# Retention on one core: scores in 64x64 products, q decayed on GpSimd, results copied by ScalarE

## The chip, the cores and the metric

One core of a Trainium2 chip. The metric is device microseconds (us) of one execution. Engines: PE is TensorE, with PEld its weight loads; DVE is VectorE, ACT is ScalarE, POOL is GpSimd; SP is SyncE, which issues all loads and stores of this kernel. Each engine works through its own instructions in the order in which the kernel emits them, and waits for the others by semaphores.

## The reference

```python
q, k, v                                   # (4, 8, 576, 64): batch, heads, positions, head size
gamma = 1 - 2.0 ** (-5 - arange(8))       # one decay for each head
scores = q @ k^T / sqrt(64)
ret = scores * where(i >= j, gamma ** (i - j), 0)
x = (ret @ v)                             # -> (2304, 512), heads side by side
h = x @ w_in                              # 512 -> 2048
y = (h * sigmoid(1.702 * h)) @ w_out      # 2048 -> 512
h2 = y @ w2_in                            # 512 -> 1024
u = h2 * softmax(h2); u = layernorm(u) * g_ln
out = u @ w2_out                          # 1024 -> 512
```

All of it in float32. The change touches the retention (up to `x`) and the order in which the weights of `w_in` and `w_out` are loaded.

## The kernel before, in words

The program works in three parts: retention, the first network (`emit_h`, `emit_y`), the second network. The change lies in the first.

*Units.* Retention is cut into 16 units: 4 batches of 4 pairs of heads. The two heads of a pair lie one in partitions 0 to 63 and one in 64 to 127 wherever the head's 64 elements are the partitions. A unit holds q and k transposed (head element by position), k and v by position, in 4 chunks of 128 positions and a last one of 64. Inside a chunk, scores are computed, masked by the triangle and multiplied with v. Between chunks, what is before is carried by a state of 64x64 for each head. The decay `gamma ** (i - j)` is split in two factors: v is scaled by `gamma ** -j` (`st0`, three ACT instructions, L304 and L305), and in the kernel before the results are multiplied by `gamma ** i` on DVE when they leave PSUM (L402 for 512 positions, L407 for the last 64).

*Steps of a unit.* `st2`: scores on PE (L351), then masked by DVE into r1 (L355, one instruction for each head). `states`: products of k and v on PE (L316), scaled on their way out by ACT (L322). `st1`: the states are accumulated over the chunks by one scan on DVE (L331). `last_scores`: scores of the last 64 positions (L339) and their mask (L340). `st4`: results from the masked scores (L372), from the states (L384, L390) and from the last positions (L395), and the two DVE instructions into x.

*Order.* It is written out by hand (`run`, L647), and the scheduler keeps it. Iteration u of the loop of L699 emits `st2(u)`, then `st4(u - 1)` with `states(u)` and `last_scores(u)` inside, the load of unit u + 4 into the buffer just freed (5 buffers, `NU`), half a weight slice if u is even, `st1(u)` and `st0(u + 2)`. In iterations 1 to 4 `split_x` cuts the first block of x into a rounded part (ACT, L423) and a rest (POOL, L424), 384 positions for each of four units.

*Weights.* Each of 8 slices of the first network comes as two halves of 512 KB in a wide format (`load_w`), is converted by 6 DVE instructions (`convert`: L226, L229, L232, twice) and split into a rounded part (ACT, L249) and a rest (POOL, two L254). This is the background work: one piece of DVE in each iteration above 3, two in even ones. The splits follow at once behind a slice's last conversion, which is in iterations 7, 11 and 15. The first network runs in three generations over its slices (0 to 2, 3 to 7, 8 to 15), each over 5 blocks of positions; the first `h` product (L443) comes in iteration 16, ahead of the last unit's `st4`.

*PSUM.* Two groups of 4 banks: one for the scores, one for states and results.

Of the kernel before, what the change touches and what calls it, by code (L numbers as in the profile page):

```python
# [13 lines left out]
ALU = mybir.AluOpType  # L14
# [3 lines left out]
B, H, S, D = 4, 8, 576, 64  # L18
NP = H // 2
# [4 lines left out]
P = 128  # L24
CH = 128
NCH = 4
# [12 lines left out]
FB = F2 // P  # L39


CQK, CQ2, CK2 = 0, NCH * 2 * CH, NCH * 2 * CH + LAST
CKN, CV = 2 * S, 2 * S + NCH * P
NV = 2 * NCH + 1
CATT = CV + NV * D
# [55 lines left out]
_M = {}  # L101
# [8 lines left out]
CMEM = _n  # L110


NU = 5
IN_AT = [_M["att"], _M["att"] + CATT] + [_M["y"] + i * CATT for i in range(3)]
ST_AT = _M["att"] + 2 * CATT
R1_AT = ST_AT + 2 * NCH * D
R2_AT = R1_AT + 4 * NCH * CH
# [30 lines left out]
class Build:  # L148
# [53 lines left out]
        lo, hi = _CC[name]  # L202
        return self.at(_M["c"] + lo, hi - lo)

    def load_unit(self, u, part=None):

        t = IN_AT[u % NU]
        a, b = {None: (0, CATT), 0: (0, 2 * CH), 1: (2 * CH, CKN), 2: (CKN, CATT), 3: (0, CKN)}[part]
        self.load(t + a, self.att_in[u, :, a:b])

    def load_raw(self, dst, src):
# [76 lines left out]
    def ybank(self, name):  # L288
        return self.ps.tile([P, 512], F32, tag="y", name=name, bufs=4)

    def q(self, t, c, rows=slice(0, P)):
        return t[rows, CQK + 2 * c * CH:CQK + (2 * c + 1) * CH] if c < NCH else t[rows, CQ2:CQ2 + LAST]

    def k(self, t, c, rows):
        return t[rows, CQK + (2 * c + 1) * CH:CQK + (2 * c + 2) * CH] if c < NCH else t[rows, CK2:CK2 + LAST]

    def st0(self, u):

# [34 lines left out]
    def last_scores(self, u, s):  # L333

        nc = self.nc
        t, _, _, r2 = self.un(u)
        for a in range(2):
            r = slice(a * D, (a + 1) * D)
            nc.tensor.matmul(s[r], self.k(t, NCH, r), self.q(t, NCH, r), start=True, stop=True)  # L339
        return lambda: nc.vector.tensor_tensor(r2, s, self.const("tri2"), ALU.mult)  # L340

    def st2(self, u):

        nc = self.nc
        t, _, r1, _ = self.un(u)
        s = [self.ybank(f"s_{u}_{a}") for a in range(2)]

        for c in range(NCH):
            for a in range(2):
                r = slice(a * D, (a + 1) * D)  # L350
                nc.tensor.matmul(  # L351
                    s[a][:, c * CH:(c + 1) * CH], self.k(t, c, r), self.q(t, c, r), start=True, stop=True
                )
        for a in range(2):
            nc.vector.tensor_tensor(  # L355
                r1[a], s[a].rearrange("r (c i) -> r c i", c=NCH),
                self.const("tri").unsqueeze(1).to_broadcast([P, NCH, CH]), ALU.mult,
            )
        if u == 0:
            self.last_scores(0, self.bank("s2")[:, 0:LAST])()  # L360

    def st4(self, u):

        nc = self.nc
        t, st, r1, r2 = self.un(u)
        o = self.bank(f"o1_{u}")
        half = [slice(a * D, (a + 1) * D) for a in range(2)]


        for c in range(NCH):  # L370
            for a, r in enumerate(half):
                nc.tensor.matmul(  # L372
                    o[r, c * CH:(c + 1) * CH],
                    t[:, CV + c * P + a * D:CV + c * P + (a + 1) * D],
                    r1[a][:, c],
                    start=(c == 0), stop=False, skip_group_check=True,
                )

        if u + 1 < B * NP:
            self.states(u + 1)  # L380

        for c in range(1, NCH):
            for r in half:
                nc.tensor.matmul(  # L384
                    o[r, c * CH:(c + 1) * CH], st[r, c - 1], self.q(t, c, r),
                    start=False, stop=(c == NCH - 1), skip_group_check=True,
                )
        o2 = self.bank(f"o2_{u}")
        for r in half:
            nc.tensor.matmul(  # L390
                o2[r, 0:LAST], st[r, NCH - 1], self.q(t, NCH, r),
                start=True, stop=False, skip_group_check=True,
            )
        for r in half:
            nc.tensor.matmul(  # L395
                o2[r, 0:LAST], t[r, CV + NCH * P:CATT], r2[r],
                start=False, stop=True, skip_group_check=True,
            )
        mask = self.last_scores(u + 1, o2[:, LAST:2 * LAST]) if u + 1 < B * NP else None
        n = NCH * CH  # L400
        d = self.const("qdec")[:, u % NP * CH:(u % NP + 1) * CH]
        nc.vector.tensor_tensor(  # L402
            self.x(u)[:, 0:n].rearrange("r (c i) -> r c i", c=NCH),
            o[:, 0:n].rearrange("r (c i) -> r c i", c=NCH),
            d.unsqueeze(1).to_broadcast([P, NCH, CH]), ALU.mult,
        )
        nc.vector.tensor_tensor(self.x(u)[:, n:S], o2[:, 0:LAST], d[:, 0:LAST], ALU.mult)  # L407
        if mask:
            mask()

# [236 lines left out]
    def run(self):  # L647
# [14 lines left out]
        def load_w():  # L662
            if raws:
                f, h = raws.pop(0)
                n = slice(h * SLICE, (h + 1) * SLICE)
                self.load_raw(self.wraw[f][:, n], self.w1_in[f][:, h * DM:(h + 1) * DM])

        for part in range(3):
            self.load_unit(0, part)
            if part == 0:  # L670
                self.load_consts()
        self.fill_scan()
        self.load_decays(0, 1)
        self.load_unit(1, 3)
        self.load_unit(1, 2)
        self.load_decays(1, NP - 1)
        for u in range(2, NU):
            self.load_unit(u, 3)
            self.load_unit(u, 2)
        load_w()  # L680
        load_w()

        for f in range(FH):
            t = T_START[f % 2]
# [5 lines left out]


        last = B * NP - 1
        self.st0(0)
        self.st0(1)
        self.st2(0)
        self.states(0)
        self.st1(0)
        self.st0(2)
        for u in range(1, last + 2):  # L699
            if u <= last:  # L700
                self.st2(u)
                if u > 3:
                    self.background(1)
            else:

                while 0 not in self.split:
                    self.background(1)
                self.emit_h(0, 0, 0, nc.vector, True)
            self.st4(u - 1)
            self.staged.add((4, u - 1))  # L710

            if u - 1 + NU <= last:
                self.load_unit(u - 1 + NU)
            if u % 2 == 0:
                load_w()
            if u <= last:
                self.st1(u)
            if u < last - 1:
                self.st0(u + 2)
            if u > 3 and u % 2 == 0:  # L720
                self.background(1)
            if u - 1 < NP:
                self.split_x(0, 0, u - 1)
# [169 lines left out]
def layout(q, k, v, moe_w_in, moe_w_out, moe2_w_in, moe2_w_out, moe2_g_ln):  # L893
# [4 lines left out]
    nat = lambda a: rows(a).transpose(0, 1, 3, 2, 4).reshape(B * NP, S, P)  # L898
    kn, vn = nat(k), nat(v)
    n = NCH * P  # L900
    chunks = lambda a: a[:, :, :n].reshape(-1, P, NCH, CH)
    qk = np.stack([chunks(tr(q)), chunks(tr(k))], 3)
    att[:, :, CQK:CQ2] = qk.reshape(-1, P, 2 * n)
    att[:, :, CQ2:CK2], att[:, :, CK2:CKN] = tr(q)[:, :, n:], tr(k)[:, :, n:]
    for at, a in ((CKN, kn), (CV, vn)):
        att[:, :, at:at + n] = a[:, :n].reshape(-1, NCH, P, P).transpose(0, 2, 1, 3).reshape(-1, P, n)
    for a in range(2):
# [35 lines left out]
```

## Time and profile before

| | |
|---|---|
| median of 3 runs | 676.5 us (676.45 to 676.79) |
| the profiled execution | 676.72 us |
| its span, first to last instruction | 674.8 us |
| PE busy | 666.7 us, 4070 products |
| PEld busy | 580.0 us |
| DVE busy | 494.4 us |
| ACT busy | 233.2 us |
| POOL busy | 235.8 us |
| moved by DMA | 49.34 MB |

The profile comes from one execution. "Busy" counts the time in which an engine works on an instruction; PE's products overlap each other in its pipeline, so that a busy PE need not be at its peak. A row of the timeline gives the start, the duration and the engine, then line, operation, what is written and read, and how many instructions were merged; in brackets the idle time before it and what ended it. A float32 product shows as two records on PE, so `x16` in L351 is 8 products.

### The profile page before, as it was taken

The page shows a single profiled execution, that of the slowest core. Times are in us where ns is not written, and L with a number is a line of the kernel's source. Part 1 is how long each engine was busy: PE and PEld are TensorE (multiplying, and loading weights), DVE is VectorE, ACT ScalarE, POOL GpSimd, SP SyncE. Part 2 cuts the span into 40 slices and gives each one's busy share as a digit, 9 for nine tenths or more (in the row PEclk, how much of TensorE's full clock was granted, in tenths as well). Part 3 has the DMA queues.
Part 4 walks back from the last instruction along what each step waited for, and adds up shares of the span by engine and source line. Part 5 has one row for each costly group of instructions (what it writes and reads, how often), then busy time and mean ns, then how long its engine had stood idle before and what let it go on. Part 6 is the DMA issues. An engine that isn't in the chain of part 4 may idle for free.

```text
span 674.8 us, 10368 instructions
## 1 busy us (share of the span) xinstructions
PE 666.7 (99%) x4070; PEld 580.0 (86%) x4070; DVE 494.4 (73%) x805; ACT 233.2 (35%) x483; POOL 235.8 (35%) x240
## 2 busy tenths in 40 slices
PE   8999999999999999999999999999999999999998
PEld 7999988899888889998888888899878888888887
DVE  3799766678877867678676675468689887887780
ACT  3554444352122224221111111255544433443331
POOL 1211476445222239521120220289844313431200
PEclk9999999999999999999999999999999999999999
DMA  8999400002213220022221200000000000000001
GB/s 325 423 378 373 180 0 2 0 1 95 93 64 115 72 63 0 1 89 69 93 64 63 64 1 0 1 0 5 1 16 32 4 29 33 31 17 17 31 32 48
DMA packets 13441, 49.34 MB, mean 73 GB/s; under 512 B 1488, under 2 KB 2384, under 8 KB 11984
## 3 DMA queue, kind: packets, MB, share of 16 engines
q1 hardware_dynamic: 13392, 48.68, 19.9%
q8 instruction: 32, 0.52, 0.3%
q14 instruction: 17, 0.14, 0.1%
HBM read 43.95 MB, written 4.72 MB: 72 GB/s over the span
## 4 chain that ended last, share of the span: by engine, by line
PE 86%; DVE 7%; issue 2%; ACT 2%; DMA 1%; POOL 0%; SPq 0%; DVEq 0%; POOLq 0%; ACTq 0%
PE h L443 28%; PE yp L473 28%; PE o L638 14%; PE h L547 10%; PE zT L611 2%; PE o L384 2%; PE s L351 1%; PE o L372 1%; DMA mem<-in_att 1%; DVE mem L331 1%; DVE mem L355 1%; DVE mem L553 1%; DVE mem L449 1%; DVE mem L586 1%; ACT gs L451 1%
## 5 line engine op out<-in xcount | busy, mean ns | idle before, releaser
L443 PE MATMUL h<-xs,w 128*128 128x512 f32 (+1 forms) x960 | 211.7, 368 | 0.4 <-POOL xs L424 0.4
L473 PE MATMUL yp<-gs,w 128*128 128x512 f32 (+1 forms) x960 | 211.0, 368 | 0.3 <-ACT gs L451 0.3
L443 PEld LDWEIGHTS h<-xs,w 128*128 128x128 f32 x960 | 175.1, 188 | 25.3 <-POOL xs L424 2.8
L473 PEld LDWEIGHTS yp<-gs,w 128*128 128x128 f32 x960 | 174.9, 188 | 23.9 <-DVE mem L481 0.7
L424 POOL TENSOR_TENSOR xs<-xb,xs 128x384 fp32r<-128x384 f32 (+3 forms) x96 | 95.2, 1018 | 228.1 <-ACT xs L423 228.1
L448 ACT ACTIVATE mem<-h 128x512 f32<-128x512 f32 (+1 forms) x80 | 44.5, 556 | 263.9 <-PE h L443 259.4
L449 DVE TENSOR_TENSOR mem<-h,mem 128x512 f32<-128x512 f32 (+1 forms) x80 | 50.9, 636 | 89.5 <-ACT mem L448 89.3
L638 PE MATMUL o<-w,zs 128*128 128x512 f32 (+1 forms) x456 | 102.9, 382 | 0.0
L638 PEld LDWEIGHTS o<-w,zs 128*128 128x128 f32 x456 | 81.3, 188 | 15.2
L254 POOL TENSOR_TENSOR w<-mem,w 128x512 fp32r<-128x512 f32 x40 | 54.7, 1394 | 67.2 <-ACT w L249 67.2
L454 DVE TENSOR_TENSOR gs<-mem,gs 128x512 fp32r<-128x512 f32 (+1 forms) x80 | 68.1, 851 | 13.0 <-ACT gs L451 6.4
L509 POOL TENSOR_TENSOR ys_s<-mem,ys_s 128x256 fp32r<-128x256 f32 x36 | 35.0, 983 | 51.9 <-ACT ys_s L508 41.8
L453 DVE CAST gs<-mem 128x512 fp32r<-128x512 f32 (+1 forms) x69 | 39.9, 578 | 6.6
L547 PE MATMUL h<-wt,ys_s 128*128 128x512 f32 x162 | 41.3, 390 | 0.0
L553 DVE TENSOR_TENSOR mem<-h,mem 128x512 f32<-128x512 f32 x36 | 24.5, 686 | 21.2 <-PE h L547 12.5
L547 PEld LDWEIGHTS h<-wt,ys_s 128*128 128x128 f32 x162 | 30.3, 188 | 6.2
L423 ACT CAST xs<-xb 128x384 fp32r<-128x384 f32 (+3 forms) x96 | 35.0, 433 | 0.0
L598 POOL TENSOR_TENSOR mem<-mem 128x1 f32<-128x1 f32 x18 | 10.3, 574 | 64.7 <-DVE mem L597 64.7
L621 DVE TENSOR_TENSOR zs<-zT,zs 128x512 fp32r<-128x512 f32 x36 | 23.1, 683 | 7.8 <-ACT zs L620 7.8
L547 PE MATMUL h<-wb,ys_a 128*128 128x512 f32 x108 | 27.6, 390 | 0.2 <-ACT mem L556 0.2
L590 DVE TENSOR_TENSOR mem<-mem 128x1024 f32<-128x1024 f32 x18 | 24.7, 1373 | 3.7 <-ACT mem L588 3.7
L232 DVE SCALAR_TENSOR_TENSOR mem<-mem 128x512 uint32<-128x512 uint32 x32 | 26.7, 833 | 0.6
(80 smaller groups left out, 729.4 us busy)
## 6 DMA issues: line engine op xcount, KB each, us to landing
mem<-in_att SPq DMA_DIRECT2D x11, 1120.0 KB, 8.5
wraw<-in_w SPq DMA_DIRECT2D x16, 512.0 KB, 10.6
mem<-in_w SPq DMA_DIRECT2D x16, 512.0 KB, 3.7
out<-mem SPq DMA_DIRECT2D x17, 256.0 KB, 2.0
mem<-in_w2in SPq DMA_DIRECT2D x8, 512.0 KB, 3.7
mem<-in_w2out SPq DMA_DIRECT2D x8, 512.0 KB, 3.7
mem<-in_att SPq DMA_DIRECT2D x5, 544.0 KB, 8.7
mem<-in_att SPq DMA_DIRECT2D x4, 576.0 KB, 9.5
```

The costliest lines, as they stand in the source:

```text
L254: nc.gpsimd.tensor_tensor(lo[:, c], w[:, c], f32(hi[:, c]), ALU.subtract)
L423: nc.scalar.copy(t[:, 0, done:done + n], x)
L424: nc.gpsimd.tensor_tensor(t[:, 1, done:done + n], x, f32(t[:, 0, done:done + n]), ALU.subtract)
L443: nc.tensor.matmul(h[:, 0:width], a[:, w], x[:, b, 0:width], start=(n == 0), stop=(n == 3 * KB - 1))
L448: nc.scalar.activation(g, h[:, 0:width], AF.Sigmoid, scale=1.702)
L449: nc.vector.tensor_tensor(g, h[:, 0:width], g, ALU.mult)
L453: nc.vector.tensor_copy(gs[:, 0], g)
L454: lo_engine.tensor_tensor(gs[:, 1], g, f32(gs[:, 0]), ALU.subtract)
L473: nc.tensor.matmul(o, a[:, w], gs[:, b], start=(first and i == 0), stop=(last and i == 2))
L509: nc.gpsimd.tensor_tensor(ys[:, 1], src, f32(ys[:, 0]), ALU.subtract)
L547: nc.tensor.matmul(o, a[:, l, k], m[:, w], start=(start and i == 0), stop=(stop and i == 5), skip_group_check=True,)
L638: nc.tensor.matmul(o[:, 0:n], z[:, a, k], b[:, c:c + n], start=(k == 0 and i == 0), stop=(k == FB - 1 and i == 2),)
```

## The change

- The scores of a chunk and head, 128 by 128, are computed as two products with 64 columns of k each, instead of one with 128. All four quarters of the array (64 rows by 64 columns) are addressed.
- q is multiplied by its decay in place before it is used (`decay_q`, two instructions): units 0 and 1 on DVE, all others on GpSimd, one unit ahead of the scores. Results then leave PSUM as plain copies on ScalarE.
- q and k lie one behind the other in a unit's input, and a unit is always loaded in two parts. There are six input buffers.
- The order of the first loads is: q and k of unit 0, decays of two pairs, constants, the rest of unit 0. Weight halves are issued behind units 2 and 4, in even iterations, and in each iteration behind the load of the last unit: five of eight slices come after that load.
- In iteration 0 (`st4(0)`) the states of unit 1 come last. Values are scaled one unit ahead up to unit 3, and two ahead from unit 5 on; iteration 3 scales units 4 and 5.

```diff
-NU = 5
-IN_AT = [_M["att"], _M["att"] + CATT] + [_M["y"] + i * CATT for i in range(3)]
+NU = 6
+IN_AT = [_M["att"], _M["att"] + CATT] + [_M["y"] + i * CATT for i in range(4)]
...
+    def decay_q(self, u, engine):
+        q = self.un(u)[0][:, CQ:CK]
+        n = NCH * CH
+        d = self.const("qdec")[:, u % NP * CH:(u % NP + 1) * CH]
+        w = q[:, 0:n].rearrange("r (c i) -> r c i", c=NCH)
+        engine.tensor_tensor(w, w, d.unsqueeze(1).to_broadcast([P, NCH, CH]), ALU.mult)
+        engine.tensor_tensor(q[:, n:], q[:, n:], d[:, 0:LAST], ALU.mult)
...
         for c in range(NCH):
-            for a in range(2):
-                r = slice(a * D, (a + 1) * D)
-                nc.tensor.matmul(
-                    s[a][:, c * CH:(c + 1) * CH], self.k(t, c, r), self.q(t, c, r), start=True, stop=True
-                )
+            for a, r in enumerate(half):
+                for w in half:
+                    k = CK + c * CH + w.start
+                    nc.tensor.matmul(
+                        s[a][w, c * CH:(c + 1) * CH], t[r, k:k + D], self.q(t, c, r),
+                        start=True, stop=True, skip_group_check=True,
+                    )
...
-        if u + 1 < B * NP:
+        if 0 < u < B * NP - 1:
             self.states(u + 1)
...
+        if u == 0:
+            self.states(1)
         mask = self.last_scores(u + 1, o2[:, LAST:2 * LAST]) if u + 1 < B * NP else None
         n = NCH * CH
-        d = self.const("qdec")[:, u % NP * CH:(u % NP + 1) * CH]
-        nc.vector.tensor_tensor(
-            self.x(u)[:, 0:n].rearrange("r (c i) -> r c i", c=NCH),
-            o[:, 0:n].rearrange("r (c i) -> r c i", c=NCH),
-            d.unsqueeze(1).to_broadcast([P, NCH, CH]), ALU.mult,
-        )
-        nc.vector.tensor_tensor(self.x(u)[:, n:S], o2[:, 0:LAST], d[:, 0:LAST], ALU.mult)
+        nc.scalar.copy(self.x(u)[:, 0:n], o[:, 0:n])
+        nc.scalar.copy(self.x(u)[:, n:S], o2[:, 0:LAST])
...
-        for part in range(3):
-            self.load_unit(0, part)
-            if part == 0:
-                self.load_consts()
+        self.load_unit(0, 0)
+        self.load_decays(0, 2)
+        self.load_consts()
+        self.load_unit(0, 1)
         self.fill_scan()
-        self.load_decays(0, 1)
-        self.load_unit(1, 3)
-        self.load_unit(1, 2)
-        self.load_decays(1, NP - 1)
-        for u in range(2, NU):
-            self.load_unit(u, 3)
-            self.load_unit(u, 2)
-        load_w()
-        load_w()
+        for u in range(1, NU):
+            for part in range(2):
+                self.load_unit(u, part)
+            if u == 1:
+                self.load_decays(2, NP - 2)
+            if u % 2 == 0:
+                load_w()
...
         last = B * NP - 1
+        self.decay_q(0, nc.vector)
         self.st0(0)
-        self.st0(1)
         self.st2(0)
+        self.decay_q(1, nc.vector)
         self.states(0)
         self.st1(0)
-        self.st0(2)
+        self.st0(1)
         for u in range(1, last + 2):
+            if u < last:
+                self.decay_q(u + 1, nc.gpsimd)
             if u <= last:
                 self.st2(u)
...
             if u - 1 + NU <= last:
-                self.load_unit(u - 1 + NU)
-            if u % 2 == 0:
+                for part in range(2):
+                    self.load_unit(u - 1 + NU, part)
+            if u % 2 == 0 or u > last - NU:
                 load_w()
             if u <= last:
                 self.st1(u)
-            if u < last - 1:
-                self.st0(u + 2)
+            for n in range(u + 1 + (u > 3), min(u + 2 + (u > 2), last + 1)):
+                self.st0(n)
```

## Rows read from the trace of the kernel before

**Rows 1.** Windows: stretch and length in us, busy us of engines, clock, DMA, GB/s.

```profile
14.52:30.39 15.87, 15.73 (x292) 14.63 (x289) 11.95 (x26) 9.51 (x23) 3.34 (x4) 1.00 1.02 422
30.39:70.39 40.00, 39.35 (x724) 36.58 (x721) 37.13 (x78) 17.94 (x40) 6.51 (x5) 1.00 0.95 373
70.39:86.98 16.59, 16.18 (x113) 14.73 (x110) 10.53 (x18) 6.90 (x16) 9.42 (x10) 1.00 0.38 133
```

**Rows 2.** Timeline of PE over one unit: start, duration in us, then what.

```profile
46.74 1.16 PE L351 MATMUL s<-mem 64*128 64x128 f32 x16
47.83 1.09 PE L372 MATMUL o<-mem 128*64 128x128 f32 x16
48.75 0.63 PE L316 MATMUL T<-mem 128*64 128x64 f32 x16
49.32 0.98 PE L384 MATMUL o<-mem 64*64 64x128 f32 x12
50.14 0.35 PE L390 MATMUL o<-mem 64*64 64x64 f32 x4
50.32 0.28 PE L395 MATMUL o<-mem 64*64 64x64 f32 x4
50.44 0.28 PE L339 MATMUL o<-mem 64*64 64x64 f32 x4
50.65 0.38 PE L351 MATMUL s<-mem 64*128 64x128 f32 x2
```

**Rows 3.** Timeline of PE at scores of units 1 and 2, and first `h`.

```profile
9.26 1.16 PE L351 MATMUL s<-mem 64*128 64x128 f32 x16 [0.55 <-DMA mem<-in_att]
...
14.52 0.72 PE L351 MATMUL s<-mem 64*128 64x128 f32 x8
...
70.39 0.45 PE L443 MATMUL h<-xs,w 128*128 128x384 f32 x1
```

**Rows 4.** Timeline of PE, up to 26.52 and up to 26.70: scores begun.

```profile
26.48 0.38 PE L351 MATMUL s<-mem 64*128 64x128 f32 x2
...
26.48 0.49 PE L351 MATMUL s<-mem 64*128 64x128 f32 x4
```

**Rows 5.** Lines up to 86 us: count, busy us, mean ns, idle before.

```profile
L402 DVE TENSOR_TENSOR xb<-o,mem 128x512 f32<-128x512 f32 x16 | 10.9, 683 | 2.6 <-PE o L384 2.6
L254 POOL TENSOR_TENSOR w<-mem,w 128x512 fp32r<-128x512 f32 x6 | 8.7, 1472 | 34.4 <-ACT w L249 34.4
L424 POOL TENSOR_TENSOR xs<-xb,xs 128x384 fp32r<-128x384 f32 x4 | 4.0, 1008 | 22.5 <-ACT xs L423 22.5
```

**Rows 6.** Timeline of ACT.

```profile
13.78 0.91 ACT L304 ACTIVATE mem<-mem 128x256 f32<-128x256 f32 x2 [1.44 <-DMA mem<-in_att]
...
25.77 0.91 ACT L304 ACTIVATE mem<-mem 128x256 f32<-128x256 f32 x2 [2.91 <-DMA mem<-in_att]
...
26.83 0.49 ACT L423 CAST xs<-xb 128x384 fp32r<-128x384 f32 x1
27.23 0.72 ACT L322 ACTIVATE mem<-T,mem 128x256 f32<-128x256 f32 x1
...
38.48 1.05 ACT L249 CAST w<-mem 128x1024 fp32r<-128x1024 f32 x1 [2.28 <-DVE mem L232]
```

**Rows 7.** Timeline of DVE around the first weight's last conversion.

```profile
35.26 0.21 DVE L340 TENSOR_TENSOR mem<-o,mem 128x64 f32<-128x64 f32 x1
35.39 0.67 DVE L331 TENSOR_TENSOR_SCAN mem<-mem 128x256 f32<-128x256 f32 x1
...
37.77 0.67 DVE L232 SCALAR_TENSOR_TENSOR mem<-wraw 128x512 uint32<-128x512 uint32 x1
...
40.19 1.24 DVE L331 TENSOR_TENSOR_SCAN mem<-mem 128x256 f32<-128x256 f32 x1 [0.88 <-ACT mem L322]
```

**Rows 8.** Timeline of POOL.

```profile
27.40 1.01 POOL L424 TENSOR_TENSOR xs<-xb,xs 128x384 fp32r<-128x384 f32 x1 [4.09 <-ACT xs L423]
39.61 2.90 POOL L254 TENSOR_TENSOR w<-mem,w 128x512 fp32r<-128x512 f32 x2 [8.52 <-ACT w L249]
```

More of the change, by code (lines that the diff above doesn't have):

```diff
@@ L39 @@
 FB = F2 // P
-CQK, CQ2, CK2 = 0, NCH * 2 * CH, NCH * 2 * CH + LAST
+CQ, CK = 0, S
 CKN, CV = 2 * S, 2 * S + NCH * P
@@ L203, in const, with load_unit @@
         return self.at(_M["c"] + lo, hi - lo)
-    def load_unit(self, u, part=None):
+    def load_unit(self, u, part):
         t = IN_AT[u % NU]
-        a, b = {None: (0, CATT), 0: (0, 2 * CH), 1: (2 * CH, CKN), 2: (CKN, CATT), 3: (0, CKN)}[part]
+        a, b = ((0, CKN), (CKN, CATT))[part]
         self.load(t + a, self.att_in[u, :, a:b])
@@ L289, in ybank, with q @@
         return self.ps.tile([P, 512], F32, tag="y", name=name, bufs=4)
[L291 to L295, printed above, removed]
+    def q(self, t, c, rows):
+        return t[rows, CQ + c * CH:min(CQ + (c + 1) * CH, CK)]
+    def decay_q(self, u, engine):
[5 more added lines that the diff above has]
+        engine.tensor_tensor(q[:, n:], q[:, n:], d[:, 0:LAST], ALU.mult)
     def st0(self, u):
@@ L338, in last_scores @@
             r = slice(a * D, (a + 1) * D)
-            nc.tensor.matmul(s[r], self.k(t, NCH, r), self.q(t, NCH, r), start=True, stop=True)
+            nc.tensor.matmul(s[r], t[r, CK + NCH * CH:CKN], self.q(t, NCH, r), start=True, stop=True)
         return lambda: nc.vector.tensor_tensor(r2, s, self.const("tri2"), ALU.mult)
@@ L346, in st2 @@
         s = [self.ybank(f"s_{u}_{a}") for a in range(2)]
+        half = [slice(a * D, (a + 1) * D) for a in range(2)]
         for c in range(NCH):
-            for a in range(2):
-                r = slice(a * D, (a + 1) * D)
-                nc.tensor.matmul(
-                    s[a][:, c * CH:(c + 1) * CH], self.k(t, c, r), self.q(t, c, r), start=True, stop=True
-                )
+            for a, r in enumerate(half):
[5 more added lines that the diff above has]
+                    )
         for a in range(2):
@@ L900, in layout @@
     n = NCH * P
[L901 to L904, printed above, removed]
+    att[:, :, CQ:CK], att[:, :, CK:CKN] = tr(q), tr(k)
     for at, a in ((CKN, kn), (CV, vn)):
```

## The prediction

> **What bounds the kernel now.** I read busy time by stretch first. [...] After 70.39 PE is nearly dense again, 16.18 of 16.59, and its work there is not changed. So the question is how far 70.39 moves. Call X_n the start of the scores of unit n on PE.
>
> Then PE in order of time over one unit [rows 2]: scores 1.09, `o` from the masked scores 0.92, states `T` 0.57, `o` from the states 0.82, then 0.18, 0.12 and 0.21 for the short ones: 3.91 us. From X_2 at 14.52 to `h` at 70.39 are 14 units [rows 3]: 55.87 us, of which 14 x 3.91 = 54.74 are products and 1.13 stalls.
>
> **The change, part by part.**
>
> *Scores as 64x64 products.* A unit's 8 products of two records each (16) become 16 products (32 records). Today records start in pairs, one of each row half: two at 26.48, and four only between 26.66 and 26.70 [rows 4]; in L372 the pair is two column halves, and a pair of 128 columns costs 0.92/8 = 0.115 [rows 2]. So rows and columns of the array can each be halved with both halves at work; no row shows both halvings fully used at once. If all four quarters run together, scores are 8 rounds of 0.115 = 0.92. A change of tile shape costs too: L339's four records take 0.21 with another shape behind them, L395's four alike 0.12 with the same, so 0.09. Scores now have L339's shape: the change between them goes, the one into L372 stays. L339 and scores: 0.12 + 0.92 + 0.09 = 1.13 instead of 0.21 + 1.09 = 1.30; 0.17 less, 3.74 a unit. Bounds: with quarters that gain nothing, 16 rounds, 0.12 + 1.84 + 0.09 = 2.05, 0.75 more; at best the second change of shape costs nothing either, 0.26 less. I take 0.17, nearest to L372's row: 14 x 0.17 = -2.4 us.
>
> A unit will have 88 records in place of 72. The trace fits 72 in 3.91 us, 54 ns each, and L395's four in 0.12, 30 ns each [rows 2]. [...]
>
> *Results copied by ScalarE (ACT).* L402 (0.68) [rows 5] and L407 leave DVE, which then is far from full, and the 1.13 us of stalls go: -1.1 (I put them down to DVE's scan, which L384 waits for and which comes late, at 40.19 [rows 7]). ACT gets a copy of 512 columns, between L423's 0.49 for 384 and L249's 1.05 for 1024 [rows 6], say 0.55, and one of 64, say 0.25: 0.8 beside some 1.7 that it has in a unit. That fits, but the copies now stand in ACT's queue ahead of the next scaling of values.
>
> *q decayed on GpSimd (POOL).* One product of 128x512 and one of 64 columns a unit. Nearest row: L254, 1.47 for 128x512 with two inputs [rows 5]; below, L424's 1.01 for 384 columns; above, 1.7, L254's pair of 2.90 less one at L254's second start. I take 1.45. Some 2 us of POOL in 3.74 would be hidden; beside POOL the scan takes 1.24 instead of 0.67 [rows 7], and DVE has room for that now. But POOL works in order, each decay stands behind what the iterations before left in its queue, and the scores of a unit now wait for it. I followed that queue:
>
> 1. X_2. Units 0 and 1 are decayed on DVE. Unit 1's q and k land at 9.26, when PE stops waiting for them [rows 3]; with 0.2 for 0.07 MB of decays moved ahead, and 0.68 for the decay, X_1 is 10.15. Then scores, L372, L384, the short ones, and unit 1's states last, two changes of shape more than in a later unit, about 4.05: 14.2. Unit 2's last part lands at 13.78 [rows 6], its q and k, half of 1.15 MB earlier at 422 GB/s, at 12.4, and 1.45 behind that is 13.9. X_2 = 14.2, -0.3.
> 2. X_3. POOL's order is decay of unit 2, `split_x` of unit 0 (L424), decay of unit 3. L424 waits for ACT: unit 1's state copy from about X_2, 0.65 (L322); the new copies 0.8; unit 2's values 1.06 (25.77 to 26.83); L423, 0.57 ahead of L424 [rows 6, 8]; then L424 1.0 and the decay 1.45: X_2 + 5.5, against 3.74. +1.75, X_3 = 19.7. While PE waits unit 1's outputs are done, so its `split_x` is early and X_4 = 23.4 without a wait.
> 3. X_5. Iteration 3 scales the values of units 4 and 5, both ahead of its L423. Unit 5's landed at 25.77 [rows 6]; two weight halves stood before it and still do (one behind unit 2, one behind unit 4), and the DMA engines were full, so no earlier. 25.77 + 1.06 + 0.57 + 1.0 + 1.45 = 29.85, against 23.4 + 3.74 = 27.15: +2.7; +1.7 if the sixth buffer, which lets SP issue this load without waiting for unit 0's outputs, brings it 1 us sooner.
> 4. X_9 and X_13. The first weight is split in iteration 7 as before: DVE's L340, no longer behind L402 and L407, at X_7 + 0.1; 37.77 - 35.26 = 2.51 to the last conversion [rows 7]; 0.71 to L249 [rows 6]; 1.13 to the two L254, 2.90 for these [rows 8]; the decay of unit 9 behind them, 1.45 less 0.2 of overlap: X_7 + 8.6, against 7.48, +1.1. The second weight does so to unit 13, +1.1; behind the third no decay is left.
>
> *Six buffers and the order of loads on SP.* Constants behind the decays, and unit 0 in two parts, are in step 1. The load of unit 15 goes out an iteration sooner, and the ten weight halves behind it follow without a wait. `h` of the first generation needs only the three slices before them. With 373 of 422 GB/s in use from 30 us on [rows 1] ACT should hardly wait for loads later: nothing.
>
> *Behind X_15.* ACT's copies of the last unit push its next `xs` casts back by about 1 us, still ahead of PE's need: nothing.
>
> Sum: -0.3 - 2.4 - 1.1 + 1.75 + 2.7 + 1.1 + 1.1 = +2.85; `h` starts at 73.2. The profiled execution took 676.72 (span 674.8 and 1.9 around it), 0.2 above the median of 676.5. Its 679.6 is 679.3 by the median.
>
> **Rivals.**
> - *POOL's queue doesn't bind* (0.17). Each wait is a sum of six or seven steps; at 1.0 a decay (L424's price) and with casts earlier, X_9 and X_13 lose most of theirs. With none: -0.3 - 2.4 - 1.1 = -3.8, 672.7. For it: POOL is busy 6.51 in 40 us [rows 1]. Against it: the rows give each step's start.
> - *Half of it binds* (0.12): gain and loss cancel, 676.5.
> - *The quarters run as pairs* (0.08), so that the change doesn't do what it says: 4.66 a unit, +10.5; POOL's waits shrink to 0.8 at X_3 and X_5 and none later: -0.3 + 10.5 - 1.1 + 1.6 = +10.7, 687.2. For it: no product of the trace lies off the diagonal; against it, row halves and column halves overlap fully.
> [...]
> - *The front end can't issue 88 records in 3.74 us* (0.01): at the 54 ns shown, 4.75 a unit, +0.84 x 14 = 11.8, 687 with the rest.
>
> **How the numbers follow.** The forecast holds 0.58, its own range 677 to 682 (a decay's price and unit 5's landing). 0.2% is 1.35 us, about what a measurement of this kernel can tell from no change: below 675.15 is faster, above 677.85 slower. Faster: the first rival and a little of the second, 0.21. Slower: most of the forecast and the last three rivals, 0.62. Same: 0.17. The range, 673 to 683, leaves out half of the first rival and most of the last three.
>
> **What would show it.** On PE: L339 to scores without the gap, and scores to L372 in about 1.0 us (2 shows pairs); units 3.74 apart, but for long waits of scores for POOL at units 3, 5, 9 and 13, of 1 to 3 us, with L424 or L254 just ahead of that decay. DVE below 35 of 40 us. If the waits are absent the queue argument is wrong; if X_5 comes by 27.5, step 3; if a decay takes 1.0, its price.

## The result and the profile after

The changed kernel takes 681.96 us (median of six runs, 680.08 to 684.48) where the kernel before, measured beside it, takes 676.59: a ratio of 1.0083, with an interval of 1.0054 to 1.0112. It is slower by some 5.4 us. The forecast was 679.3, and the range 673 to 683 holds the median. The profiled execution took 680.08, 3.36 more than the one of before. Three of the six runs lay at 683.25 to 684.48 with a mean clock of 0.992 to 0.995; the profile of one such run stands under `c_again`. So what follows accounts for the 3.4 us of the profiled run, the lowest of the six, and not by itself for the 5.4 of the medians.

The first `h` product starts at 73.99 in place of 70.39, 3.60 later, and behind it the two kernels are alike again. So the stage that the prediction looked at holds the whole difference of the two profiled runs. The same three stretches as in [rows 1], changed kernel (length, busy PE, PEld, DVE, ACT, POOL, clock, DMA share, GB/s):

```profile
15.56:33.12 17.56, 15.52 (x355) 14.23 (x354) 11.04 (x19) 13.01 (x33) 10.77 (x12) 1.00 1.02 419
33.12:73.99 40.87, 37.67 (x891) 34.94 (x887) 31.64 (x55) 24.28 (x59) 21.39 (x23) 1.00 0.89 344
73.99:90.58 16.59, 16.17 (x112) 14.74 (x110) 8.59 (x14) 8.33 (x20) 10.00 (x10) 1.00 0.37 128
```

PE has some 2.0 us without work in the first stretch and 3.2 in the second, 5.2 together, where it had 0.14 and 0.65. DVE has gone from 37.13 of 40.00 to 31.64 of 40.87. The time didn't go into longer products. One unit of PE's timeline, to be held against [rows 2]:

```profile
29.47 1.10 PE L359 MATMUL s<-mem 64*64 64x128 f32 x32 [1.28 <-POOL mem L300]
30.51 1.09 PE L381 MATMUL o<-mem 128*64 128x128 f32 x16
31.43 0.64 PE L322 MATMUL T<-mem 128*64 128x64 f32 x16
32.00 0.98 PE L393 MATMUL o<-mem 64*64 64x128 f32 x12
32.82 0.35 PE L399 MATMUL o<-mem 64*64 64x64 f32 x4
33.00 0.28 PE L404 MATMUL o<-mem 64*64 64x64 f32 x4
33.12 0.22 PE L345 MATMUL o<-mem 64*64 64x64 f32 x2
33.12 0.33 PE L359 MATMUL s<-mem 64*64 64x128 f32 x2
...
44.92 0.99 PE L393 MATMUL o<-mem 64*64 64x128 f32 x12 [1.23 <-DVE mem L337]
...
61.55 0.99 PE L393 MATMUL o<-mem 64*64 64x128 f32 x12 [1.75 <-DVE mem L337]
```

From the first of the sixteen 64x64 products to L381 it is 1.04 us (30.51 less 29.47; before, 1.09 for eight products), and the last scores and the next unit's scores now start together at 33.12: no change of shape between them. A unit without a stall is 3.65 to 3.70 us. What the units lost stands in the brackets, and it is of two kinds. The waits of PE between 14 and 74 us, changed kernel (us in total, times, longest):

```profile
PE o L393 <- DVE mem L337: 3.0, 2, 1.8
PE s L359 <- POOL mem L300: 2.0, 2, 1.3
PE o L381 <- issue: 0.2, 1, 0.2
```

Scores wait for the decay on POOL at units 3 and 5; the outputs from the states, L393, wait for DVE's scan, L337, behind X_8 and X_12, just ahead of X_9 and X_13. The starts of scores: X_1 10.19, X_2 15.56, X_3 20.56, X_4 24.21, X_5 29.47, X_6 33.12, X_8 40.52, X_9 46.05, X_12 57.15, X_13 62.68, `h` 73.99.

The start of the stage brought one more loss. Windows of 1 us around units 1 and 2, changed kernel (clock third from the end):

```profile
10.00:11.00 1.00, 0.81 (x28) 0.81 (x32) 0.68 (x3) 0.73 (x2) 0.00 (x0) 0.99 1.04 416
11.00:12.00 1.00, 1.00 (x18) 0.67 (x12) 0.81 (x2) 0.91 (x3) 0.00 (x0) 0.50 1.02 421
12.00:13.00 1.00, 1.00 (x14) 0.97 (x10) 0.77 (x2) 0.00 (x0) 0.39 (x1) 0.50 1.02 420
13.00:14.00 1.00, 1.00 (x10) 0.70 (x8) 0.00 (x0) 0.00 (x0) 0.95 (x2) 0.50 1.12 402
```

The granted clock is 0.50 in three of these windows, and L381 at 11.40, behind unit 1's scores, takes 1.97 us there, against 1.09 at 30.51, where the clock is 1.00. At the start L322 had waited 1.78 us and these scores 0.46. Before, the clock was 1.00 from 10 to 15 us.

### The profile page after: what moved, and what is told of

Same layout as the page of the kernel before. It is cut to its first block, busy times and chain, and to the rows that moved or that the text cites. A ratio compares the mean times of both kernels' runs of the same rounds, so it can differ in the third digit from the quotient of the medians.

```text
span 678.3 us, 10984 instructions
## 1 busy us (share of the span) xinstructions
PE 665.0 (98%) x4326; PEld 578.0 (85%) x4326; DVE 488.8 (72%) x777; ACT 243.7 (36%) x515; POOL 260.1 (38%) x268
## 4 chain that ended last, share of the span: by engine, by line
PE 88%; DVE 5%; ACT 3%; issue 2%; POOL 1%; DMA 1%; SPq 0%; POOLq 0%; DVEq 0%; ACTq 0%
PE h L449 28%; PE yp L479 28%; PE o L644 14%; PE h L553 10%; PE zT L617 2%; PE o L393 2%; PE o L381 2%; PE s L359 1%; DMA mem<-in_att 1%; DVE mem L337 1%; DVE mem L559 1%; PE T L322 1%; POOL xs L430 1%; DVE mem L592 1%; DVE mem L518 1%
## 5 line engine op out<-in xcount | busy, mean ns | idle before, releaser
L430 POOL TENSOR_TENSOR xs<-xb,xs 128x384 fp32r<-128x384 f32 (+3 forms) x96 | 96.1, 1027 | 213.4 <-ACT xs L429 213.4
L254 POOL TENSOR_TENSOR w<-mem,w 128x512 fp32r<-128x512 f32 x40 | 53.8, 1372 | 53.3 <-ACT w L249 41.5
```

What stands on the lines that cost most here:

```text
L254: nc.gpsimd.tensor_tensor(lo[:, c], w[:, c], f32(hi[:, c]), ALU.subtract)
L430: nc.gpsimd.tensor_tensor(t[:, 1, done:done + n], x, f32(t[:, 0, done:done + n]), ALU.subtract)
```

## The experiments

Theory of the first ones: PE's stalls are POOL's decays, put behind `split_x` at units 3 and 5, and a chain ACT to DVE to PE at units 9 and 13, which the trace after shows in place of the one that I had written. The rival: the stalls at 9 and 13 are POOL's decay behind two L254 all the same.

**`c_again`: the changed kernel, unchanged.**

> The changed kernel once more, unchanged, as the yardstick of this chip. Its six runs so far fall in two groups, 680.1 to 680.7 with a mean clock of 0.997 to 1.000 and 683.3 to 684.5 with 0.992 to 0.995. Theory (waits in GpSimd's and ScalarE's queues, and PE's clock falling in the idle they leave): both groups again, and a run at 0.992 to 0.995 shows a second stretch at half clock behind one of the waits of units 3, 5, 9 or 13. Rival (the clock has nothing to do with it, the chip's load does): no stretch at half clock behind a wait.

Measured: 681.91 (681.34 to 683.79), ratio 1.0079 [1.0066, 1.0092]. The group at 680 did not come again. The profile is of the run at 683.79. PE's timeline at unit 5 and in the last unit, and the windows at unit 5:

```profile
29.95 1.98 PE L359 MATMUL s<-mem 64*64 64x128 f32 x32 [1.92 <-POOL mem L300]
...
75.89 0.62 PE L322 MATMUL T<-mem 128*64 128x64 f32 x14 [0.82 <-issue]
```

```profile
28.00:30.00 2.00, 0.08 (x6) 0.05 (x4) 1.05 (x2) 2.00 (x7) 2.00 (x3) 0.97 1.03 416
30.00:32.00 2.00, 2.00 (x34) 1.67 (x36) 1.12 (x3) 0.44 (x2) 2.00 (x3) 0.50 1.02 420
32.00:34.00 2.00, 2.00 (x32) 1.97 (x32) 1.86 (x3) 0.00 (x0) 2.00 (x3) 0.67 1.01 416
```

Here the wait at X_5 was 1.92 instead of 1.28 (ACT had to wait 0.52 for unit 5's values), the clock fell to 0.50 behind it, and the scores took 1.98 instead of 1.10: X_6 comes at 35.16 in place of 33.12. So the clock can fall at X_5, in a run of the same kernel. It is not all of the difference: the first `h` comes at 77.78, 3.79 later than in the first profile. 2.04 of that is there at X_6, and 1.55 is added behind X_14, where the clock is 1.00 and PE stands idle on issue (the line at 75.89). What that idle time is stands under `c_al_warm`. The other runs at 0.992 to 0.995 have no profile.

**`b_scores64`: the kernel before with 64x64 scores alone.**

```
-                nc.tensor.matmul(s[a][:, chunk], self.k(t, c, r), self.q(t, c, r), start=True, stop=True)
+                for w in (slice(0, D), slice(D, 2 * D)):
+                    nc.tensor.matmul(s[a][w, chunk], self.k(t, c, r)[:, w], self.q(t, c, r), ...)
```

> The kernel before with one part of the change alone: scores as 64x64 products. Theory A (four quarters run together, 0.2 us a unit less on PE): VectorE, at 37.1 of 40 us before, becomes the bound, some 3.75 to 3.85 us a unit instead of 3.91 and the stalls: h some 1 to 2 us sooner, 675. Theory B (PE's instructions arrive in pieces of 16 KB by the same DMA engines that the loads keep full, and with 176 instead of 144 a unit they arrive late now and then): PE gaps of about 1 us that end on nothing the profile shows, each 1 to 2 us behind an instruction transfer, take the gain back: 676.5 to 677.5. Before, with 144 a unit, there was no such gap.

Measured: 676.80 (675.76 to 680.64), ratio 1.0016 [1.0004, 1.0029]: no gain. The profile is of the lowest of the twelve runs, 675.76; five took 677.73 to 680.64, four of them with a mean clock of 0.999 or more, and have no profile. In it units of 3.70 begin as in the changed kernel and `h` comes at 69.52, 0.87 earlier than before, not 14 x 0.21 = 2.9: from 30.39 to `h` DVE is busy 36.46 of 39.13 us and PE waits three times, 1.3 us in all, for the scan. A shorter unit alone meets DVE, and, as the count under `c_al_warm` shows, late instructions too. The median lies in the range that the second theory gave; how much each takes in such a run is not shown.

**`c_scores128`: the changed kernel with 64x128 scores.**

```
-                for w in half:
-                    k = CK + c * CH + w.start
-                    nc.tensor.matmul(s[a][w, c * CH:(c + 1) * CH], t[r, k:k + D], ...)
+                k = CK + c * CH
+                nc.tensor.matmul(s[a][:, c * CH:(c + 1) * CH], t[r, k:k + CH], ...)
```

> The changed kernel with the scores by 64x128 products again, the other two parts of the change kept. Units without a stall are 3.91 instead of 3.70. If the stalls of the changed kernel are set by the other engines (GpSimd's decay, the chain over ACT and DVE to the scan), four units that are 0.21 longer take some 0.8 out of each of the two stalls at units 9 and 13 and 0.2 out of those at units 3 and 5: 16 x 0.21 = 3.4 longer, 2.0 of it given back, first h near 75.4, about 683.4. Rival (the smaller products cost time of their own beyond this, through late instructions, in the changed kernel as it stands): no more than 682 and a first h at 74 or earlier.

Measured: 683.17 (682.68 to 683.90), 1.0099 [1.0085, 1.0113]; first `h` at 75.92. PE's timeline at unit 8:

```profile
45.78 0.98 PE L391 MATMUL o<-mem 64*64 64x128 f32 x12 [1.33 <-DVE mem L337]
```

Units are 3.91, and the steps to X_9 and X_13 take 5.32, a stall of 1.41 instead of 1.83: the chain behind the stall doesn't run on PE, so a longer unit hides more of it, though 0.42 a stall and not the 0.8 that was expected. By the profiled runs (682.68 and 680.08) the 64x64 scores are worth 2.6 us here, by the medians 1.2. The rest of the change costs 6.8 alone (683.17 less 676.34, the kernel before beside it); no run takes its copies, decays and order of loads apart.

**`c_ahead`: decay two units ahead.**

```
+        self.decay_q(2, nc.gpsimd)
         for u in range(1, last + 2):
-            if u < last:
-                self.decay_q(u + 1, nc.gpsimd)
+            if u < last - 1:
+                self.decay_q(u + 2, nc.gpsimd)
```

> Changed kernel, but q is decayed two units ahead on GpSimd, so that no decay stands behind the xs rests or the weight rests of the iterations before it. Theory (the queue of GpSimd makes scores of units 3 and 5 late): the two waits of scores for the decay, 0.76 and 1.28 us of PE, go or shrink to the landing of the loads, h starts 1 to 2.5 us sooner; the waits of L393 for the scan at units 7 and 11 stay at 1.2 and 1.8 us: about 679 (678 to 680) against 680.3 of the changed kernel's faster group. Rival A (decays behind the weight rests decide units 9 and 13, as first predicted): those waits go too, another 3 us, 676. Rival B (ScalarE's copies are what is late): nothing moves.

Measured: 679.98, 1.0053 [1.0041, 1.0065]. The waits at units 3 and 5 are gone, X_5 is 27.12 instead of 29.47. So both were the decay's place in POOL's queue. But 2.35 us of it were not kept: `h` is at 74.02, because PE now stands idle at other places, ended by nothing that the profile shows ("issue", 3.1 us in all). By the medians it is 1.9 below `c_again`, measured beside it.

**`c_late`: the weight's split at the end of an iteration.** `background(1, False)` still converts between scores and outputs, but leaves a split that is due; `background(0)` emits it at the end of the iteration, so that the cast L249 stands behind the state copy in ACT's queue.

```
-                    self.background(1)
+                    self.background(1, False)
...
                 self.split_x(0, 0, u - 1)
+            self.background(0)
```

> Changed kernel, but a weight's split (ScalarE's cast, then two GpSimd rests) is emitted at the end of iterations 7, 11 and 15, behind the state copy, the result copies and the scan, not ahead of them. Theory (the cast holds up ScalarE's state copy and result copies, behind these VectorE's mask of the last scores and the scan): the waits of L393 at 44.9 and 61.6 go, about 3.5 us; but the decays of units 9 and 13 then stand behind later weight rests, and scores of these units wait for GpSimd instead, some 2 us each: 680 or so, no gain. Rival A (GpSimd's rests slow the scan to 1.8 us and that is all): L393 still waits, since the scan still runs beside GpSimd; 680, without long waits of scores. Rival B: 677, no new wait.

Measured: 687.94 (682.15 to 690.78), 1.0159 [1.0123, 1.0196], the slowest of all. PE's waits up to 90 us:

```profile
PE s L359 <- POOL mem L300: 9.3, 4, 2.9
```

and three of the windows, with the clock:

```profile
28.00:31.00 3.00, 1.56 (x30) 1.56 (x32) 2.14 (x3) 1.95 (x6) 2.71 (x4) 0.57 1.02 420
31.00:34.00 3.00, 3.00 (x41) 2.67 (x36) 1.89 (x3) 0.00 (x0) 3.00 (x4) 0.50 1.03 423
...
48.00:52.00 4.00, 2.14 (x34) 1.82 (x36) 2.48 (x3) 0.39 (x2) 4.00 (x6) 0.61 1.02 409
```

No wait for the scan is left, as the theory wanted; in its place scores wait for the decay at units 9 and 13, behind L254, and the clock falls behind both (0.61 from 48 to 52 us, 0.50 from 70 to 73) and behind the wait at unit 5 (0.50 from 31 to 34). The rival's chain exists as well. In this run the clock stayed at 1.00 from 10 to 15 us, and X_2 was 13.92 in place of 15.56. But none of these 1.64 us were kept: X_5 is 29.44 (29.47 in the changed kernel). ACT waits there for the landing of unit 5's values, and starts on them at 25.71; the wait of scores at unit 5 is longer than before by what the start had gained.

**`c_mask_first`: the mask ahead of the copies.** The last scores and the short outputs lie in one PSUM bank, and the mask of the one (DVE) is queued behind the copy of the other (ACT): in the changed kernel, at unit 8, it waited 2.27 us for that copy.

```
-        nc.scalar.copy(self.x(u)[:, 0:n], o[:, 0:n])
-        nc.scalar.copy(self.x(u)[:, n:S], o2[:, 0:LAST])
         if mask:
             mask()
+        nc.scalar.copy(self.x(u)[:, 0:n], o[:, 0:n])
+        nc.scalar.copy(self.x(u)[:, n:S], o2[:, 0:LAST])
```

> The changed kernel, with one edit: the mask of the last scores (DVE) is issued ahead of the two copies of x (ACT) that read the same PSUM bank. Theory (at units 9 and 13 the outputs wait for the scan, the scan stands behind that mask, and the mask stands behind the copies): the mask comes 0.6 to 0.85 us earlier (the copies take 0.64 and 0.21), the two waits of the outputs shrink by about 0.6 each from 1.8, the first h comes near 72.8 instead of 73.99, about 680.7 against 681.96. Rival (the scan is late because of GpSimd's two weight halves, whatever stands ahead of it): the waits stay at 1.7 to 1.8 and the time within 0.3 of 681.96. Late instructions (the transfers of 16 KB seen in the runs before) could take back a part: then PE has gaps that end on issue where the waits were, and the time lies between.

Measured: 683.58 (681.80 to 683.98), 1.0106 [1.0091, 1.0122]. The time that was expected is missed. The profile, of the run at 681.80, has the clock's fall behind X_5 (0.59 and 0.56 from 30 to 34 us; X_6 at 35.31, against 33.12), so its unit 8 starts 2.19 later than the changed kernel's. Its DVE, then POOL, then PE at that unit:

```profile
43.03 0.23 DVE L346 TENSOR_TENSOR mem<-o,mem 128x64 f32<-128x64 f32 x1 [0.50 <-PE o L345]
44.28 1.23 DVE L337 TENSOR_TENSOR_SCAN mem<-mem 128x256 f32<-128x256 f32 x1 [1.02 <-ACT mem L328]
```

```profile
43.69 2.90 POOL L254 TENSOR_TENSOR w<-mem,w 128x512 fp32r<-128x512 f32 x2 [7.68 <-ACT w L249]
46.55 1.09 POOL L300 TENSOR_TENSOR mem<-mem 128x512 f32<-128x512 f32 x1
```

```profile
45.57 0.99 PE L393 MATMUL o<-mem 64*64 64x128 f32 x12 [0.21 <-DVE mem L337]
...
47.69 1.10 PE L359 MATMUL s<-mem 64*64 64x128 f32 x32 [0.72 <-POOL mem L300]
```

The mask no longer waits for ACT, and L393 waits 0.21 instead of 1.23. But the scores of unit 9 now wait 0.72 for the decay behind L254. The steps to X_9 and X_13 shrink from 5.53 to 4.98 each: 1.1 us in all, and less than the two waits that the edit shortened, because the second chain ends only some half a microsecond earlier than the first. Behind X_14 two idle times on issue, 0.48 and 0.32, cost it another 0.8. Against the profile of `c_again`, which has the same fall at unit 5, X_14 comes 1.26 earlier (67.36 and 68.62). The median is not lower than that of `c_again`, and its clock is 0.992 to 0.997 against 0.995 to 0.997; with four runs I can't say more.

**`c_ahead_late`: both together.** The edits of `c_ahead` and `c_late` in one.

> Both at once: q two units ahead, and the weight's split behind the iteration's copies and scan. Theory: neither wait is left, units are 3.70 apart from unit 6 on; against the changed kernel's faster group of 680.3, 2 us for units 3 and 5 and 3.5 us for units 9 and 13: 675 (673.5 to 676.5), below the kernel before. Rival (the two effects overlap, one only takes the place of the other): 678 or more.

Measured: 679.71, 1.0053 [1.0041, 1.0065]: nothing better than `c_ahead`, and not what was expected. POOL's waits are gone and the scan's are 0.4 in all, yet units take up to 5.05 us. An example, PE's rows in order of time:

```profile
58.43 0.59 PEld L322 LDWEIGHTS T<-mem 128*64 128x64 f32 x15
58.54 0.63 PE L322 MATMUL T<-mem 128*64 128x64 f32 x15
...
60.25 0.13 PEld L322 LDWEIGHTS T<-mem 128*64 128x64 f32 x1 [1.23 <-issue]
60.26 0.27 PE L322 MATMUL T<-mem 128*64 128x64 f32 x1 [1.09 <-issue]
```

PE stops in the middle of a loop of 16 alike records, and its wait ends on nothing that the profile shows. The trace has a 16 KB transfer on the instruction queue from 57.97 to 58.99; others like it end at 39.84 and 52.03, and PE resumes at 41.29 and 53.54. I took it that PE's instructions arrive late while the DMA engines are full (share 1.02 here), and that 88 records a unit run into it where 72 did not. Three runs were made on that.

**`c_al_scores128`: that kernel with 64x128 scores** (the edit of `c_scores128`).

> Changed kernel with q two units ahead and the split behind, but with the scores as 64x128 products again (88 records a unit back to 72). Theory B (late instructions): the PE gaps of 0.6 to 1.3 us at T, L381 and inside the scores (28.8, 29.8, 40.5, 52.3, 59.0, 65.7 with 64x64) are gone, units 3.87 to 3.91 apart throughout, h at 70.5 to 71.5 in spite of the longer scores: 677.5 (676.5 to 678.5), faster than the 679.7 with 64x64. Rival (the gaps come from loads or from ScalarE): the gaps stay, and with 0.2 us a unit more it is slower, 681 to 682.

Measured: 677.18, 1.0012 [1.0003, 1.0020]. From X_6 to `h` every unit takes 3.91 and no idle time ends on issue: 2.5 us faster with the longer products.

**`c_al_held`: that kernel with nine weight halves issued late, by ScalarE.** They go out three at a time in iterations 14 to 16, instead of one in each iteration from 11 on by SP.

```
-            if u % 2 == 0 or u > last - NU:
+            if u % 2 == 0 and u <= last - NU + 1:
...
+            for _ in range(3 if u > 13 else 0):
+                load_w(nc.scalar)
...
```

> Changed kernel with q two units ahead and the split behind; of the weight halves that came behind the last unit's load, nine are held back and issued by ScalarE in iterations 14 to 16. Between 54 and 66 us the DMA engines then carry little. Theory B: PE's gaps at 52.3, 59.0 and 65.7 vanish (the instruction transfers there find free DMA engines), the ones at 29 and 40 stay: 3 us less, 676.5 (675.5 to 678). Rival (the instruction front end is too slow by itself, or something else): gaps stay, 679.5 or more.

Measured: 678.17, 1.0036 [1.0024, 1.0048]. The idle time at 52 and at 66 us is gone and that at 59 shrank to 0.72; those before 45 us, where the engines are as full as ever (DMA share 1.02 from 20 to 50 us), stay.

**`c_al_warm`: that kernel with twelve products on zeros at the start.**

```
+        for _ in range(9):
+            nc.tensor.matmul(wb[:, 0:P], warm, warm, start=True, stop=True)
         self.states(0)
+        for _ in range(3):
+            nc.tensor.matmul(wb[:, 0:P], warm, warm, start=True, stop=True)
```

> Changed kernel with q two units ahead and the split behind; twelve more products on zeros on PE (nine while the values of unit 0 land, three behind the states of unit 0), which touch nothing else. Theory (PE idles 2.4 us at 6.7, and its clock falls to half for 3 to 4 us from about 10): the clock stays at 1.00 from 5 to 16 us, L381 of unit 0 takes 0.92 and not 1.9, X_2 comes at 13.9 to 14.2 instead of 15.3, and h 1.2 to 1.5 us sooner: 678.4. Rival (X_2 waits for unit 2's q anyway): X_2 stays at 15.3, 679.7.

Measured: 680.04, 1.0051 [1.0039, 1.0063]. The clock is 1.00 from 10 to 15 us (before that edit it was 0.50 from 10 to 12) and X_2 comes at 14.68 instead of 15.28, but five idle times on issue, 4.0 us in all, take it back, and `h` is at 74.37.

These runs fit late instructions. `b_scores64` seems not to: it has the same 88 records, its DMA engines are as full (98.8% of 16 to 60 us, here 101.4%), and of its idle time only 0.2 us end on issue. A count in the traces settles it. Number PE's instructions in order of start, the products' records, their weight loads and its few semaphore instructions alike. Between 14 and 80 us, eight runs have 27 idle times on issue, and each ends within two records of the same places of the program: 961, 1217, 1473 and so on, 256 apart. Each also ends 1.2 to 1.7 us behind the end of a 16 KB transfer. The page of the changed kernel has 34 transfers of 16 KB on the instruction queue for PE's 8652 records and loads, that of the kernel before 32 for 8140: some 254 to a transfer in both. So PE's instructions come in blocks of 256, and PE waits for the next block.

How often a block is needed follows from the unit: 88 records and their 88 weight loads use up 256 instructions in 256/176 x 3.70 = 5.4 us, 72 in 256/144 x 3.91 = 7.0. In `c_ahead_late`, from instruction 961 to 2497, a block's transfer starts 3.4 to 4.4 us behind the first instruction of the block before, takes 0.9 to 1.0, and PE goes on 1.3 to 1.7 behind it: a block every 5.8 to 6.7 us, too slow for 88 and fast enough for 72. In `c_al_scores128` PE reaches each block from 705 on 2.7 us or more behind its transfer. `b_scores64` stands at the same limit: seven of its nine blocks from 705 to 2753 start 1.2 to 1.55 us behind their transfer, but its units are longer by the waits for the scan, so little idle time shows. In `c_al_held`, once the loads are thin (DMA share 0.36 from 60 to 70 us), the transfers start 0.2 and 1.4 us behind the block before, and PE doesn't wait.

**`c_best128` and `c_best_mixed`: what helped, together.** Decay two ahead, split at the end, products on zeros, mask first, values scaled one ahead for two units longer, 64x128 scores; in the second also the nine late halves by ScalarE, and 64x64 scores for units 13 to 15.

```
-            for n in range(u + 1 + (u > 3), min(u + 2 + (u > 2), last + 1)):
+            for n in range(u + 1 + (u > 5), min(u + 2 + (u > 4), last + 1)):
```

> All that the runs showed put together: decay two units ahead, weight split at the end of a unit, twelve products on zeros in the idle time at the start, mask ahead of the copies, the values' scaling one unit ahead for two units longer, and the scores by 64x128 products. Theory (72 records a unit leave no late instructions, and no other wait is left): X_2 near 14.6, every unit 3.91 to 3.96 from there, first h at 69.5 (before: 70.39), about 675.8. Rival (something else is next, as the step at unit 5 of 4.51 in the run with 64x128 scores): first h at 70.1 to 70.7, 676.5 to 677.

> As the one before, with the nine late weight halves issued by ScalarE in units 14 to 16, and the scores of units 13 to 15 by 64x64 products, when the transfers have thinned out. Theory (the smaller products gain 0.21 a unit where instructions arrive in time): three units of 3.70, first h at 68.9, about 675.2. Rival (the smaller products lose there too, or the late issue delays the rest): units 13 to 15 of 3.91 or more, 675.8 or more.

Measured: 676.13, 0.9994 [0.9985, 1.0003], and 675.74, 0.9993 [0.9984, 1.0001]. Window of the second, from 15.57 to `h`:

```profile
15.57:69.28 53.71, 53.71 (x1054) 50.17 (x1050) 43.14 (x73) 39.46 (x92) 30.97 (x34) 1.00 0.90 360
```

PE has no idle time left there. Its steps around the smaller products, from X_12 to X_15, are 3.71, 3.69 and 3.70, and `h` comes at 69.28 (70.37 in `c_best128`, later than expected, since X_2 was 15.41). Both undo the loss; what each part gives in them was not measured one by one. Neither is shown to be faster than the kernel before: the intervals hold 1.

## Why the prediction was right, and where it was not

The terms, forecast against the profiled run (us on the start of `h`): X_2 -0.3, came +1.04; scores 14 x -0.17, came 14 x -0.21 = -2.9; old stalls -1.1, booked as -1.1 (see *DVE's stalls*); X_3 +1.75, came +1.30; X_5 +2.7, came +1.56; X_9 and X_13 +1.1 each, came +1.83 each; a last unit of 3.91 instead of 3.70, +0.2; two units of 3.65, -0.1. Sum +2.85 and +3.6.

That the sums lie only 0.75 apart is in part luck. X_2, the two late stalls and the last unit came 3.0 worse than forecast; scores, X_3, X_5 and the short units 2.2 better. The other 1.9 us, from the profiled run to the median, are in none of the terms. In `c_again`, the one longer run with a profile, it is the clock falling behind a wait, and late instructions.

- *Scores.* The four quarters do run together: 32 records in 1.04 to the next group, 3.70 a unit against 3.74. The rival of pairs (4.66) is out. So is the front end's 54 ns a record: 88 in 3.70 are 42 ns. That PE is kept from its records in another way, by blocks of instructions that arrive late, I had nowhere. In the profiled run it is 0.2 us.
- *DVE's stalls.* DVE fell below 35 of 40 us, as forecast, but the term of -1.1 had a wrong reason. The scan at 40.19 [rows 7] was not late because DVE was full: DVE stood idle for 0.88 until ACT's state copy, and that stood behind the cast L249 of 38.48 [rows 6]. Kernel before, ACT, then PE:

```profile
39.44 0.72 ACT L322 ACTIVATE mem<-T,mem 128x256 f32<-128x256 f32 x1
```

```profile
41.49 0.99 PE L384 MATMUL o<-mem 64*64 64x128 f32 x12 [0.44 <-DVE mem L331]
```

So 0.51 of the 1.13 (4.42 from X_8 to X_9, less 3.91) was the chain of X_9 in a smaller form. Freeing DVE did not take it away, and it grew.
- *X_2.* The working was right and the clock missing: 13.92 where the clock held (`c_late`), 15.56 where it fell. For `h` it hardly counts, since X_5 is the same in both.
- *X_3.* The mechanism is the forecast one, step by step. ACT, then POOL, changed kernel:

```profile
15.66 0.74 ACT L328 ACTIVATE mem<-T,mem 128x256 f32<-128x256 f32 x1 [3.75 <-PE T L322]
16.18 0.64 ACT L412 COPY xb<-o 128x512 f32<-128x512 f32 x1
16.72 0.21 ACT L413 COPY xb<-o 128x64 f32<-128x64 f32 x1
16.82 0.92 ACT L310 ACTIVATE mem<-mem 128x256 f32<-128x256 f32 x2
...
17.87 0.50 ACT L429 CAST xs<-xb 128x384 fp32r<-128x384 f32 x1
...
40.69 1.05 ACT L249 CAST w<-mem 128x1024 fp32r<-128x1024 f32 x1 [2.23 <-DVE mem L232]
41.64 0.72 ACT L328 ACTIVATE mem<-T,mem 128x256 f32<-128x256 f32 x1
42.15 0.64 ACT L412 COPY xb<-o 128x512 f32<-128x512 f32 x1
42.68 0.21 ACT L413 COPY xb<-o 128x64 f32<-128x64 f32 x1
```

```profile
18.45 1.01 POOL L430 TENSOR_TENSOR xs<-xb,xs 128x384 fp32r<-128x384 f32 x1 [4.49 <-ACT xs L429]
19.41 1.10 POOL L300 TENSOR_TENSOR mem<-mem 128x512 f32<-128x512 f32 x1
...
41.81 2.51 POOL L254 TENSOR_TENSOR w<-mem,w 128x512 fp32r<-128x512 f32 x2 [5.31 <-PE s L359]
44.28 1.48 POOL L300 TENSOR_TENSOR mem<-mem 128x512 f32<-128x512 f32 x1
```

State copy, two copies, values, cast, L430, decay: X_2 + 5.0 against + 5.5. Most of the difference is the decay's price, 1.10 and not 1.45; over all fourteen it is 1.28, and 1.48 at 44.28, behind L254.
- *X_5.* 29.47 against 29.85, and in part for another reason. I had unit 5's values land at 25.77 and hold up the chain. In the profiled run ACT started them at 25.75 without waiting for any transfer: it had come from the result copies at 24.12 and unit 4's values at 24.70. There the queue of ACT set the start; where ACT was earlier or the load later, it was the landing (25.71 in `c_late`, 26.22 in `c_again`). `c_ahead` took the wait away.
- *X_9 and X_13: the step that failed.* Place and existence were right; what I put there, "the decay of unit 9 behind" two L254, is not what PE waited for. ACT's cast L249 comes at 40.69, ahead of the state copy (ACT above). The state copy, at 41.64, and the copies behind it come late; DVE's mask waits for the second of these, and the scan stands behind the mask:

```profile
42.92 0.22 DVE L346 TENSOR_TENSOR mem<-o,mem 128x64 f32<-128x64 f32 x1 [2.27 <-ACT xb L413]
43.07 1.80 DVE L337 TENSOR_TENSOR_SCAN mem<-mem 128x256 f32<-128x256 f32 x1
```

The scan ends at 44.87, and L393 starts at 44.92. The decay of unit 9 ended at 45.76, just ahead of X_9 at 46.05. `c_late` and `c_mask_first` show both chains, one a little behind the other: with the first shortened, 1.28 a stall is left (4.98 less 3.70), against the 1.1 forecast for the second. I had written that the new copies stand in ACT's queue, and followed that to the values alone, not to the mask that shares their bank. Held against the kernel before, where the state copy also ends some 5.6 us behind X_7, the 1.83 are four parts: 0.51 that stood there already, 0.54 by which the scan starts later (6.25 behind X_7 against 5.71), 0.56 by which it takes longer (1.80 against 1.24), and 0.22 by which the shorter unit wants it sooner.
- *The scan's price.* With no POOL work beside it a scan takes 0.67 to 0.69 in both profiles. The one at 43.07 takes 1.80 and the one at 59.71 1.78, each beside the second L254 (43.05 to 44.32 for the first) and 0.59 us of the decay behind it; I knew 1.24, beside the two L254 of the kernel before. But at 76.33 a scan beside an L254 takes 0.68, and there it is the L254 that takes 1.74 instead of 1.28. What makes the one or the other longer is not shown.
- *The clock.* The forecast gave its fall at X_5 a chance of 0.04 and 3.7 us; no run shows 3.7. It fell there in some of the runs and cost some 1.6 (5.21 from X_5 to X_6 in `c_again`, 3.65 in the profiled run), in `c_late` 2.6 (6.21), and it fell at the start in the profiled run (0.50 from 11 to 14 us). It should have had more weight: I forecast idle times longer than any before, and in `c_again` and `c_late` it fell behind the longest of them (1.92 and 2.88 us).

## What to carry to other kernels

Work moved to an idle engine is cheap only if its place in that engine's queue is: here the decays on POOL kept scores waiting 0.76 and 1.28 us at units 3 and 5. Follow each moved instruction to everything that shares a buffer or a bank with it, and look for the second chain that ends just behind the first: removing one of two gains only their difference. Read what ended an engine's idle time before calling that engine the bound: the scan that came late was itself kept waiting by ACT (0.88 us in the kernel before). Cutting a product in two also doubles the instructions that have to be brought in for it (32 records a unit for the scores instead of 16). A bound engine that is made shorter meets the next limit at once (in `b_scores64` DVE, busy 36.46 of 39.13 us), so price the stalls that the slack had hidden, and price an idle time on TensorE with the clock that it may cost (some 1.6 and 2.6 us at X_5 in `c_again` and `c_late`).

## What was not expected of the hardware

- TensorE idle on issue in the middle of a loop, 0.2 to 1.1 us each and 3.5 us in all in `c_ahead_late`, none from unit 6 on in `c_al_scores128`. The idle times end at places of the program that lie multiples of 256 instructions apart, each 1.2 to 1.7 us behind a transfer of 16 KB on the instruction queue. The changed kernel has it as well: 0.2 us in the first profile, 2.5 in that of `c_again`.
- Sixteen 64x64 products over four quarters of the array take 1.04 us to the next group, against 1.09 for eight of 64x128. The other 0.16 of the 0.21 went where the last scores stood: they took 0.21 ahead of the next scores, and now start together with them, at 33.12.
- The granted clock fell to 0.50 behind waits of 1.92 (`c_again`) and 2.88 us (`c_late`) in this stage, and stayed at 1.00 behind others of 1.23, 1.28 and 1.75 (changed kernel). At the start it fell behind 1.05 and 0.42 (`c_ahead`) and stayed behind 1.46 and 0.47 (`c_late`): the length of a wait alone doesn't say whether it falls.
